# A 32-byte pad behind one small gate tile, so that every tile placed after it starts at a multiple of 64 bytes

## Chip, cores and metric

The kernel runs on one core of a Trainium2 chip. The metric is the device time of one execution in microseconds; less is better.

## The reference, cut to what matters

Three stages run one after the other on float32 data: block-causal attention, a mixture of experts whose gate is normalised by eight rounds of row and column scaling, and a "soft" mixture with 4 slots for each of 8 experts.

```python
scores = scale * np.matmul(q, k.transpose(0, 1, 3, 2))          # 4 x 8 heads, 576 x 64
attn = softmax over the allowed 64-blocks; x = attn @ v          # x becomes 2304 x 512
...
P = np.exp(logits)                                               # logits = x @ w_gate, 2304 x 8
for _ in range(8):
    P /= P.sum(1, keepdims=True) + 1e-09
    P /= P.sum(0, keepdims=True) + 1e-09
    P *= N / E
for e in range(E):
    out += P[:, e:e + 1] * (np.maximum(x @ w1[e], 0.0) @ w2[e])  # w1: 512 x 1024, w2: 1024 x 512
...
slot_input = softmax over tokens(x @ phi).T @ x                  # 32 slots
slot_out[e] = np.maximum(slot_input[e] @ w1[e], 0.0) @ w2[e]
result = softmax over slots(x @ phi) @ slot_out
```

## The kernel before

**Precision.** Matmul operands are split in two: a value rounded to the fp32r type (name ending in h) and the rest (ending in l). A product is three matmuls, h by h, h by l and l by h, into one PSUM tile.

**Stages.** Attention for 16 head pairs comes first, and the first expert matmuls fill its gaps (`fill`). The experts are cut into 32 units u of 256 hidden columns. Units 0 to 3 go plainly (`L1` at L173 to L175, `L2` at L196). For units 4 to 30 a loop at L928 runs per unit:

- `L1S` twice, for the token chunks (0, 1) and (2, 3) of 512 tokens: the first layer by a scheme with seven products instead of eight. Each product is six matmuls of 512 columns at L832. In the trace they write `A..` or `S..` and read as moving operand either tiles of x (`xh`, `xl`) or the sums of x tiles that were formed once, `T..`. Three of the seven products, S2 by T2, S3 by T3 and A22 by T4, read `T`. The stationary operand is the prepared weight tile `es`.
- `L1P` for chunk 4 of 256 tokens: 24 matmuls of 256 columns at L880 to L882.
- `L2` for all 18 token tiles: six matmuls of 512 columns each at L196. The moving operand is the weight tile `w2h` or `w2l`, the stationary one 128 tokens of the hidden tiles `hh` and `hl`. There are two sets of hidden tiles, hA in pool `ua` and hB in pool `pb`. Chunks 0, 2 and 4 use hA, chunks 1 and 3 use hB. The result is added into `acc` by VectorE at L212.

`inter` (L889) weaves these by a written pattern: pieces of `L1S` or `L1P` of the present step between pieces of `L2` of the step before. Unit 31 goes the same way, and its second layer is woven with the third stage.

**Where tiles lie.** SBUF is given out pool by pool, and every tile takes a multiple of 32 bytes on a partition. Pool `gp` holds `P` (576 bytes), `m1` (32), `rs` (96) and `cs` (32). The pools opened later lie behind it: those of the attention stage, and, in the same place once attention is over, pool `pb`. The addresses in the compiled program:

| tiles | first byte | remainder by 64 |
|---|---|---|
| xh, xl (moving at L832, L880 to L882) | 4352 to 73984 | 0 |
| w1h, w1l, w2h, w2l, also used for es | 78080 to 110848 | 0 |
| hh, hl of set hA | 114944, 119040 | 0 |
| acc of chunks 0 to 2 | 123136 to 143616 | 0 |
| P, cs | 147712, 148416 | 0 |
| pool pb: acc of chunks 3 and 4 | 148448 to 156640 | 32 |
| pool pb: T (12 tiles), tmp | 160736 to 222176 | 32 |
| pool pb: hh, hl of set hB | 193504, 197600 | 32 |
| attention: kh, kl, qs, PT, v, pe | 158560 to 209632 | 32 |

The slices that the matmuls take of these tiles start a multiple of 512 bytes behind the tile's start in all of `xh`, `xl`, `T`, `es`, `w2` and `hh`, so that they keep the remainder.

Of the kernel before, what the change touches and what calls it, by code (L numbers as in the profile page):

```python
# [7 lines left out]
F32 = mybir.dt.float32  # L8
# [9 lines left out]
N, DM, E, F = 2304, 512, 8, 1024  # L18
# [16 lines left out]
def attn_moe_softmoe_kernel(ctx: ExitStack, tc: tile.TileContext, qk1, q, k, v, wg, w1, w2, phi, m2w1, m2w2, cst, out):  # L35
# [5 lines left out]
    gp = ctx.enter_context(tc.tile_pool(name="gp", bufs=1))  # L41
# [227 lines left out]

    m1 = gp.tile([128, 1], F32, name="m1")  # L270
    rs = gp.tile([128, NT], F32, name="rs")
    cs = gp.tile([128, E], F32, name="cs")
    gl = {}
    mbt = [None]

# [1082 lines left out]
```

## Time and profile before

| | us |
|---|---|
| median of 3 runs | 1843.0 |
| lowest and highest | 1839.62, 1845.62 |
| the profiled execution, its own time | 1843.25 |
| its span in the profile | 1841.5 |

The span runs from the first to the last instruction of the profiled execution; the time lies 1.75 us above it. The mean granted clock of TensorE was 0.994 of full speed. In the chain of work a piece's duration is the time that it adds to the chain, from one start to the next; the "mean ns of one" of the groups is the span of a single matmul in the pipeline and overlaps with its neighbours.

### The profile page before, as it was taken

The numbers are of one execution on the slowest core, as the hardware profiler recorded it, in microseconds if no ns is written. First come the engines' busy times: TensorE is split into PE (matmuls) and PEld (weight loads), VectorE is DVE, ScalarE is ACT, GpSimd is POOL, SyncE is SP. The second block draws the span as 40 slices with busy tenths as digits, with TensorE's granted clock in tenths as the row PEclk, the third lists the DMA queues.
The fourth block names the chain that finished last, engine by engine and source line by source line (L and its number), as shares of the span: only waits on it lengthen the run. The fifth ranks groups of instructions, "written<-read, shape, count | busy, mean of one in ns | idle before, by whom it ended". The sixth has DMA issues, their size and how long they took to land.

```text
span 1841.5 us, 24675 instructions
## 1 busy us (share of the span) xinstructions
PE 1801.7 (98%) x9239; PEld 1443.7 (78%) x9239; DVE 1257.5 (68%) x2469; ACT 578.9 (31%) x1475; POOL 300.6 (16%) x416
## 2 busy tenths in 40 slices
PE   6999999998999999999999999999999999999997
PEld 4777777777888888888888888888888888888764
DVE  7878777479766666666666666666667666666542
ACT  4667656323222222222222222222222222222222
POOL 6546343433000000000000000000000000000010
PEclk9999999999999999999999999999999999999999
DMA  5533322010000000000000000000000000000877
GB/s 182 155 113 109 98 78 72 24 41 29 23 23 24 23 24 23 21 16 23 23 24 23 24 24 23 24 23 23 23 24 23 16 20 23 23 24 23 296 269 273
DMA packets 81095, 108.23 MB, mean 59 GB/s; under 512 B 4688, under 2 KB 55632, under 8 KB 80976
## 3 DMA queue, kind: packets, MB, share of 16 engines
q1 hardware_dynamic: 80976, 106.66, 17.8%
q8 instruction: 73, 1.20, 0.3%
q14 instruction: 46, 0.38, 0.1%
HBM read 101.92 MB, written 4.72 MB: 58 GB/s over the span
## 4 chain that ended last, share of the span: by engine, by line
PE 91%; DVE 4%; DMA 2%; POOL 1%; ACT 1%; issue 1%; SPq 0%; ACTq 0%; POOLq 0%; DVEq 0%
PE l L196 42%; PE S L832 17%; PE A L832 12%; PE pvp L551 3%; PE l L882 2%; PE l L880 2%; PE l L881 2%; PE tp L519 1%; PE l L173 1%; PE l L175 1%; PE l L174 1%; DMA r<-in_moe_w_dram 1%; PE s L442 1%; PE h L1177 1%; PE s L443 1%
## 5 line engine op out<-in xcount | busy, mean ns | idle before, releaser
L212 DVE SCALAR_TENSOR_TENSOR acc<-l,P,acc 128x512 f32<-128x512 f32 x504 | 378.1, 750 | 222.6 <-PE l L196 221.2
L196 PE MATMUL l<-w2h,hl 128*128 128x512 f32 x1132 | 446.5, 394 | 6.1 <-DVE hl L836 5.6
L196 PE MATMUL l<-w2h,hh 128*128 128x512 f32 x1132 | 451.7, 399 | 0.6 <-ACT hh L177 0.6
L196 PE MATMUL l<-w2l,hh 128*128 128x512 f32 x1132 | 446.9, 395 | 0.0
L847 DVE TENSOR_TENSOR tmp<-S,tmp 128x512 f32<-128x512 f32 x275 | 185.0, 690 | 144.4 <-PE S L832 141.4
L196 PEld LDWEIGHTS l<-w2h,hl 128*128 128x128 f32 x1132 | 213.4, 189 | 56.9 <-DVE hl L836 5.8
L196 PEld LDWEIGHTS l<-w2h,hh 128*128 128x128 f32 x1132 | 214.1, 189 | 45.5 <-ACT hh L177 1.0
L196 PEld LDWEIGHTS l<-w2l,hh 128*128 128x128 f32 x1132 | 213.7, 189 | 41.8
L835 ACT ACTIVATE hh<-tmp 128x512 fp32r<-128x512 f32 x216 | 136.6, 632 | 302.4 <-DVE tmp L847 269.8
L806 POOL TENSOR_TENSOR st<-r 128x256 f32<-128x256 f32 x56 | 40.6, 746 | 1032.6 <-DMA r<-in_moe_w_dram 1032.6
L832 PE MATMUL S<-T,es 128*128 128x512 f32 x660 | 171.8, 396 | 0.0
L832 PE MATMUL A<-xh,es 128*128 128x512 f32 x440 | 154.2, 391 | 0.0
L832 PE MATMUL S<-xh,es 128*128 128x512 f32 x440 | 154.1, 391 | 0.0
L836 DVE SCALAR_TENSOR_TENSOR hl<-tmp,hh 128x512 fp32r<-128x512 f32 x216 | 147.9, 685 | 0.1
L832 PEld LDWEIGHTS S<-T,es 128*128 128x128 f32 x660 | 124.0, 188 | 29.0
L694 ACT ACTIVATE es<-r 128x256 fp32r<-128x256 f32 x112 | 46.4, 417 | 228.0 <-PE l L881 227.2
L694 ACT ACTIVATE es<-st 128x256 fp32r<-128x256 f32 x112 | 46.4, 414 | 214.0 <-PE S L832 132.1
L832 PEld LDWEIGHTS S<-xh,es 128*128 128x128 f32 x440 | 82.6, 188 | 18.6
L119 ACT ACTIVATE w2h<-r 128x256 fp32r<-128x256 f32 x160 | 54.2, 407 | 136.1 <-PE l L196 127.4
L832 PEld LDWEIGHTS A<-xh,es 128*128 128x128 f32 x440 | 82.6, 188 | 18.0
L847 DVE TENSOR_TENSOR tmp<-A,tmp 128x512 f32<-128x512 f32 x110 | 75.9, 690 | 18.3 <-PE A L832 16.6
L832 PE MATMUL S<-xl,es 128*128 128x512 f32 x220 | 86.3, 392 | 0.0
(239 smaller groups left out, 2786.7 us busy)
## 6 DMA issues: line engine op xcount, KB each, us to landing
r<-in_moe_w_dram SPq DMA_DIRECT2D x80, 512.0 KB, 3.5
mw<-in_moe_w_dram SPq DMA_DIRECT2D x64, 512.0 KB, 6.6
kraw<-in_k_dram SPq DMA_DIRECT2D x16, 576.0 KB, 3.9
qraw<-in_q_dram SPq DMA_DIRECT2D x16, 576.0 KB, 4.3
v<-in_v_dram SPq DMA_DIRECT2D x16, 256.0 KB, 3.0
out_dram<-ob SPq DMA_DIRECT2D x6, 512.0 KB, 3.1
qk<-in_qk_dram SPq DMA_DIRECT2D x4, 512.0 KB, 6.9
out_dram<-ob SPq DMA_DIRECT2D x6, 256.0 KB, 2.3
```

The lines of the kernel that those rows point to most:

```text
L119: p = [nc.scalar.activation(out=h, in_=r[:, a:a + 256], func=AF.Copy)]
L196: nc.tensor.matmul(o, lh, w[:, kf, :], start=(m == 0), stop=(m == 5))
L212: nc.vector.scalar_tensor_tensor(out=av, in0=o, scalar=P[:, tt, e:e + 1], in1=av, op0=ALU.mult, op1=ALU.add)
L551: nc.tensor.matmul(o[64 * a:64 * a + 64, lo:hi], w, r(a), start=(m == 0), stop=(m == len(its) - 1))
L694: nc.scalar.activation(out=h, in_=src, func=AF.Copy),
L806: nc.gpsimd.tensor_tensor(out=o, in0=a, in1=b, op=alu)
L832: nc.tensor.matmul(o[:, 0:H_], a[:, k], b[:, k], start=(k == 0 and m == 0), stop=(k == 1 and m == 2))
L835: nc.scalar.activation(out=h, in_=src, func=AF.Relu)
L836: nc.vector.scalar_tensor_tensor(out=lo, in0=src, scalar=0.0, in1=f32(h), op0=ALU.max, op1=ALU.subtract)
L847: nc.vector.tensor_tensor(out=out, in0=o, in1=i, op=ALU.add)
L880: nc.tensor.matmul(o[:, 0:n], wh, xhv, start=(kt == 0), stop=False)
L881: nc.tensor.matmul(o[:, 0:n], wh, xlv, start=False, stop=False)
```

## The change

The tile `cs` is allocated with 16 instead of 8 float32 columns, and the kernel uses the first 8. It takes 64 instead of 32 bytes, so that every tile allocated behind it starts 32 bytes later. The remainder by 64 becomes 0 for all tiles of the last four rows of the table. No instruction, no order and no size of an operand is changed.

```diff
     m1 = gp.tile([128, 1], F32, name="m1")
     rs = gp.tile([128, NT], F32, name="rs")
-    cs = gp.tile([128, E], F32, name="cs")
+    cs = gp.tile([128, 2 * E], F32, name="cs")[:, 0:E]
     gl = {}
```

## Rows read from the trace of the kernel before

**Rows 1.** The page: busy time and share of the span of TensorE.
```profile
PE 1801.7 (98%) x9239; PEld 1443.7 (78%) x9239; DVE 1257.5 (68%) x2469; ACT 578.9 (31%) x1475; POOL 300.6 (16%) x416
```

**Rows 2.** The page: the chain that ended last, by engine.
```profile
PE 91%; DVE 4%; DMA 2%; POOL 1%; ACT 1%; issue 1%; SPq 0%; ACTq 0%; POOLq 0%; DVEq 0%
```

**Rows 3.** Windows: width, then busy time of each engine, PEclk, DMA share, GB/s.
```profile
440.00:450.00 10.00, 8.04 (x39) 6.57 (x37) 10.00 (x11) 3.06 (x6) 6.66 (x6) 1.00 0.16 52
450.00:455.00 5.00, 1.32 (x3) 1.13 (x4) 5.00 (x8) 0.96 (x2) 3.63 (x4) 0.57 0.00 0
...
600.00:1000.00 400.00, 400.00 (x1840) 330.17 (x1839) 275.67 (x460) 95.66 (x204) 24.07 (x33) 1.00 0.07 22
```

**Rows 4.** Waits of PE: us in total, times, longest.
```profile
PE l L196 <- DVE hl L836: 5.6, 1, 5.6
```

**Rows 5.** Chain of work through one unit, 907.40 to 954.55: start, us, what.
```profile
907.40 1.39 PE A L832 x6
908.78 1.40 PE S L832 x6
910.18 1.37 PE l L196 x6
911.55 1.40 PE S L832 x6
912.96 1.39 PE l L196 x6
914.34 1.36 PE S L832 x6
915.70 2.76 PE A L832 x12
918.46 1.39 PE S L832 x6
919.85 1.36 PE A L832 x6
921.21 1.40 PE S L832 x6
922.61 2.75 PE l L196 x12
...
929.50 1.37 PE S L832 x6
930.87 2.79 PE l L196 x12
...
937.82 1.40 PE A L832 x6
939.22 1.39 PE S L832 x6
940.61 0.12 PE l L880
...
941.32 2.75 PE l L196 x12
...
948.24 2.80 PE l L196 x12
...
954.55 1.39 PE A L832 x6
```

**Rows 6.** Groups by line and shape: busy us, mean ns of one, idle before.
```profile
L212 DVE SCALAR_TENSOR_TENSOR acc<-l,P,acc 128x512 f32<-128x512 f32 x504 | 378.1, 750 | 222.6 <-PE l L196 221.2
...
L832 PE MATMUL S<-T,es 128*128 128x512 f32 x660 | 171.8, 396 | 0.0
...
L832 PE MATMUL S<-xh,es 128*128 128x512 f32 x440 | 154.1, 391 | 0.0
...
L832 PE MATMUL A<-T,es 128*128 128x512 f32 x330 | 86.0, 396 | 0.0
...
L443 PE MATMUL s<-kl,qs 128*128 128x512 f32 x32 | 12.9, 402 | 0.0
```

## Prediction

> **What bounds the kernel now.** Read the busy shares first: TensorE is busy for 98% of the span, VectorE for 68% [rows 1]. A busy share alone doesn't say that TensorE sets the end, so the chain that ended last comes next: 91% of it lies on TensorE [rows 2]. The windows say where. Between 600 and 1000 us TensorE is busy for 400.00 of 400 us, VectorE for 275.67, and DMA takes 0.07 of its engines [rows 3]. In this long stretch nothing but the rate of back-to-back matmuls counts. At the changeover near 450 us it is another matter: VectorE is busy throughout, TensorE for 1.32 of 5 us [rows 3], and the one long wait of the second layer, 5.6 us, falls on VectorE [rows 4].
>
> A change that moves addresses alone can act only through the time of single instructions, so the last view is the chain through one unit, piece by piece [rows 5]. All its pieces of 512 columns are six matmuls or twelve, and still they don't take the same time. The reader is to sort them by the remainder of the operands' addresses. The settled best is 1.36 us for six (914.34 and 919.85, both on x tiles), 226.7 ns a matmul. The pieces that read T, whose tiles begin 32 bytes past a multiple of 64, take 1.40 us (908.78, 911.55, 921.21, 937.82, one more alike, and the second half of the piece at 915.70). Twelve matmuls with a stationary operand out of hB, which lies off by 32 too, take 2.79 or 2.80 (930.87, 948.24, and one more of each), while twelve out of hA take 2.75 even in the worst places. Pieces whose own operands are aligned, but which follow a piece that reads T or hB, take 1.37 to 1.39 (907.40, 910.18, 912.96, 918.46, 939.22, 954.55): the disturbance wears off over some six matmuls.
>
> The groups say the same of one matmul: 396 ns where T is read, 391 where xh is [rows 6].
>
> **How much an offset costs, and what it looks like.** 1.40 less 1.36 over six is 6.7 ns a matmul. Between a matmul of 256 columns, 0.12 us (940.61), and one of 512, 226.7 ns, lie 107 ns, 0.417 ns a column. So 6.7 ns is the time of 16 columns, 64 bytes of float32. A row of 512 columns is 2048 bytes; read in pieces of 64 bytes it touches 32 from an aligned start and 33 from 32 bytes past it. That is an inference from these rows; they show only the price.
>
> [...]
>
> **The change, part by part.** It adds and removes no instruction. What it moves is the start of everything in pool pb and of the attention tiles, to remainder 0.
>
> *One unit.* I put the settled time on every piece that is now disturbed, and let pieces alone whose disturbance has another cause. Such a cause is there: hA pieces right behind matmuls of 256 columns take 2.75 instead of 2.72 (941.32 and one more), with aligned operands on both sides. The hB pieces in the same place (948.24 and one more) should then fall from 2.80 to 2.75 and not to 2.72. The terms:
> - six pieces that read T, 1.40 to 1.36: 6 x 0.04 = 0.24 us;
> - hB in the first place (930.87 and one more), 2.79 to 2.72: 0.14;
> - hB behind 256 columns, two pieces: 0.10;
> - aligned pieces behind T: 910.18 0.01, 912.96 0.03, 918.46 0.03, 939.22 0.03, and two pieces of twelve (922.61 and one more, 2.75 to 2.72) 0.06, in all 0.16;
> - aligned pieces behind or ahead of hB: 907.40 0.03, 929.50 and one more 0.01 each, in all 0.05.
>
> The sum is 0.69 us of the unit's 47.15 (907.40 to 954.55).
>
> *All units.* The loop has 27 such units: 27 x 0.69 = 18.6 us. As a check, 660 and 330 matmuls read T [rows 6], that is 165 pieces of six, 27.5 units' worth. Unit 31 has its six T pieces as well, with followers: 0.24 + 0.16 = 0.4 us.
>
> *Does it reach the end?* In this stretch TensorE has no gaps that could swallow it [rows 3]. What is late next is VectorE: it has 275.67 of 400 us to do, and with TensorE 1.5% faster 394 us for it, 70%. The adds into acc take 750 ns [rows 6] for every six second-layer matmuls, half of the 1.36 us that those take. VectorE, ScalarE and GpSimd get no time credited.
>
> *Attention.* Its score matmuls read kh, kl and qs, all off by 32. Only the 64 of 512 columns (L442 and L443, 32 each) can be set beside a like shape: 402 ns against 391 [rows 6], 64 x 11 ns = 0.7 us. The other 320 are narrower; from below they gain nothing, from above 11 ns each, 3.5 us. TensorE isn't alone on the chain there, and the changeover behind it hangs on VectorE [rows 3, 4]; I take 0.5 us for the stage, nearer to the lower end, and keep 0 and 4.2 for the range.
>
> *Sum.* 18.6 + 0.4 + 0.5 = 19.5 us off the profiled execution's 1843.25: 1823.75. The median of the runs is 0.25 us lower than that execution, so 1823.5 us, 1.06% less.
>
> **The rivals.**
>
> *The pieces are slow for where the tiles lie, not for the remainder.* All slow tiles lie at 148448 bytes or above, and every fast fp32r operand of 512 columns lies below, so the trace can't part the two by itself. Against it: the excess is the time of 64 bytes, and T tiles spread over 62 kB show the same 1.40. If it holds, the time stays at 1843.2 us, give or take 3. [...]
>
> *Only one of the two operands matters for its remainder.* T is moving, hB is stationary. If only T gains, a unit gives 0.24 + 0.16 = 0.40 us, and 27 units 10.8: with unit 31's 0.4 the time is 1831.8. If only hB does, 0.14 + 0.10 + 0.05 = 0.29 a unit, 7.8 us: 1835.2. For it speaks that the two enter by different reads; against it that both show the same excess, 2.80 less 2.75 where the place is the same and 1.40 less 1.36.
>
> *Slower: the clock gives way in the long stretch.* At the changeover the granted clock fell to 0.57 in a 5 us window in which TensorE was busy for 1.32 us [rows 3]; so a fall by half is to be had in this kernel. From 600 to 1000 us it is 1.00. [...] From (19.5 + 5.5) x 2 = 50 us of lower clock on, the kernel would be measurably slower, 1849 us or more. Against it: TensorE is already busy throughout that stretch, at full clock.
>
> **How the numbers follow.** This kernel can show a difference of 0.3%, 5.5 us. I give the full gain 0.80, the gain of one operand alone 0.10, no change 0.06, the clock 0.04. The first two are faster by more than 5.5 us, so faster is 0.90, same 0.06, slower 0.04. The range: at the low end attention gives its 4.2 instead of 0.5 us, 1843.0 - 18.6 - 0.4 - 4.2 = 1819.8, and 1819 with the rounding of the pieces; at the high end it takes in the case that only T gains, 1832, and 1833 with the same allowance. Both together hold some 8 in 10, since the full case can also miss by more than the pieces' rounding (0.005 us in each of some 20 pieces of 27 units, up to 2.7 us if all err the same way).
>
> **What would show it right or wrong.** In the chain through one unit: the pieces that read T at 1.36, those of hB at 2.72 and, behind 256 columns, 2.75, those behind T at 1.36, the unit at about 46.46 us. The group of S on T at 391 ns instead of 396. VectorE's adds into acc still at 750 ns. T pieces still at 1.40 would make the remainder the wrong cause; hB at 2.79 beside T at 1.36 would mean that only the moving operand counts; a unit of 46.46 and a time that hasn't fallen by some 19 us would mean that the gain is lost at the changeover or behind unit 31.

## The result, and the profile after

The changed kernel takes 1824.14 us in the median of 4 runs (1821.59 to 1826.4), the kernel before 1843.57 beside it. The ratio is 0.9897, with a 95% interval of 0.9873 to 0.992: 1.0% faster. The forecast was 1823.5 us.

The chain of work through one unit of the changed kernel, 897.90 to 944.38 us (start, us, what); it answers to [rows 5]:

```profile
897.90 1.36 PE A L832 x6
899.26 1.36 PE S L832 x6
...
904.70 1.36 PE S L832 x6
906.06 2.72 PE A L832 x12
...
912.86 2.72 PE l L196 x12
...
921.02 2.72 PE l L196 x12
...
927.82 1.36 PE A L832 x6
...
931.25 2.75 PE l L196 x12
...
938.17 2.75 PE l L196 x12
...
944.38 0.68 PE A L832 x3
```

Every piece of six in this unit takes 1.36 us now, with T or without (899.26 and 927.82 read T), every piece of twelve 2.72, with hA (912.86) or hB (921.02). Behind matmuls of 256 columns both take 2.75 (931.25 hA, 938.17 hB). The unit lasts 46.48 us instead of 47.15.

The groups by line and shape of the changed kernel, against [rows 6] (busy us, mean ns of one, idle before):

```profile
L212 DVE SCALAR_TENSOR_TENSOR acc<-l,P,acc 128x512 f32<-128x512 f32 x504 | 377.9, 750 | 212.8 <-PE l L196 212.4
...
L832 PE MATMUL S<-T,es 128*128 128x512 f32 x660 | 167.3, 389 | 0.0
...
L832 PE MATMUL S<-xh,es 128*128 128x512 f32 x440 | 153.3, 389 | 0.0
...
L443 PE MATMUL s<-kl,qs 128*128 128x512 f32 x32 | 12.8, 401 | 0.0
```

T and xh are alike at 389 ns (391 was forecast; the matmuls on xh that follow T were disturbed before and are in that mean), VectorE's add is unmoved at 750, and so, all but 1 ns, is the score matmul of the attention stage (402 before).

The span fell by 21.7 us, to 1819.8, more than the medians did. Three lines of each chain say where: the 30 second-layer matmuls near 384 us, the first A piece of the loop, and the first of unit 31. Before:

```profile
384.06 9.47 PE l L196 x30
...
462.24 1.39 PE A L832 x6
...
1709.00 1.39 PE A L832 x6
```

After:

```profile
384.17 6.93 PE l L196 x30
...
459.15 1.39 PE A L832 x6
...
1688.06 1.36 PE A L832 x6
```

The loop, from its first A piece to unit 31, takes 1228.91 us instead of 1246.76, 17.85 less, and what comes behind takes 0.8 less. The other 3.1 us were gained ahead of the loop, 2.5 of them by the 30 matmuls (6.93 instead of 9.47). That is the clock, in the windows from 380 us on, before and after (width, busy times, PEclk, DMA share, GB/s):

```profile
380.00:390.00 10.00, 6.84 (x21) 5.38 (x21) 7.29 (x19) 2.36 (x7) 3.95 (x4) 0.66 0.08 29
```

```profile
380.00:390.00 10.00, 6.74 (x33) 5.56 (x32) 8.79 (x22) 2.36 (x7) 4.27 (x4) 1.00 0.11 41
```

The first of these two is of before. There the clock granted was 0.66 in that stretch: 0.50 from 384 to 388 us, after TensorE had waited for 3.16 us, with a matmul of 512 columns started every 0.426 us. This execution of the changed kernel kept 1.00 behind a wait of 3.26 us, with one every 0.227, and why isn't shown. It is the fastest of its four runs; the medians, 19.4 us apart, don't rest on it.

### The profile page after: what moved, and what is told of

Same layout as the page of the kernel before. It is cut to its first block, busy times and chain, and to the rows that moved or that the text cites. A ratio compares the mean times of both kernels' runs of the same rounds, so it can differ in the third digit from the quotient of the medians.

```text
span 1819.8 us, 24675 instructions
## 1 busy us (share of the span) xinstructions
PE 1779.8 (98%) x9239; PEld 1441.5 (79%) x9239; DVE 1255.9 (69%) x2469; ACT 579.4 (32%) x1475; POOL 301.7 (17%) x416
## 4 chain that ended last, share of the span: by engine, by line
PE 89%; DVE 3%; POOL 1%; DMA 1%; ACT 1%; issue 1%; SPq 0%; ACTq 0%; DVEq 0%; POOLq 0%
PE l L196 42%; PE S L832 16%; PE A L832 12%; PE pvp L551 2%; PE l L882 2%; PE l L881 2%; PE l L880 2%; PE l L173 1%; PE tp L519 1%; PE l L175 1%; DMA r<-in_moe_w_dram 1%; PE l L174 1%; PE h L1177 1%; PE s L442 1%; PE s L443 1%
## 5 line engine op out<-in xcount | busy, mean ns | idle before, releaser
L832 PE MATMUL S<-T,es 128*128 128x512 f32 x660 | 167.3, 389 | 0.0
L832 PE MATMUL A<-xl,es 128*128 128x512 f32 x220 | 85.6, 389 | 0.0
```

The lines of the kernel that those rows point to most:

```text
L832: nc.tensor.matmul(o[:, 0:H_], a[:, k], b[:, k], start=(k == 0 and m == 0), stop=(k == 1 and m == 2))
```

## The experiments

In all of them "lower tiles" are x, the weights with es, and hA; "upper tiles" are T, tmp and hB. Unless it is said otherwise, the edit is shown against the changed kernel. Remainders by 256 are those of the tiles' addresses in the compiled programs.

### Upper tiles 64 bytes past a multiple of 128

```diff
-    cs = gp.tile([128, 2 * E], F32, name="cs")[:, 0:E]
+    cs = gp.tile([128, 4 * E], F32, name="cs")[:, 0:E]
```

> The pad is 96 bytes instead of 32, so that T, hB and the attention tiles start 64 bytes past a multiple of 128 (in the changed kernel all of them start at multiples of 128). Theory (a piece of 64 bytes is what counts): T pieces 1.36 us, hB 2.72 and 2.75, unit 46.48, time 1822 to 1826. Rival (the boundary is 128 bytes): T pieces 1.40, hB 2.79 to 2.80, unit about 47.15, time about 1843.

Measured: 1844.53 us, ratio to before 1.0008 (0.9999 to 1.0017). All upper tiles start at multiples of 64, and nothing is gained. Chain:

```profile
908.08 1.39 PE A L832 x6
909.47 1.39 PE S L832 x6
...
931.61 2.80 PE l L196 x12
```

The piece on T (909.47) takes 1.39, that on hB (931.61) 2.80; the unit 47.20. So in this kernel a multiple of 64 is not enough, against the prediction's reading. 128 was the rival written down; the next pair of runs shows that it isn't a multiple of anything that is wanted.

### Lower tiles off, and all tiles off

```diff
-    wg_raw = const.tile([128, KD, E], F32, name="wg_raw")
+    wg_raw = const.tile([128, KD * E + 8], F32, name="wg_raw")[:, 0:KD * E].rearrange("p (k e) -> p k e", k=KD)
```

This puts 32 bytes ahead of all lower tiles. With `cs` at its old 32 bytes the upper ones come to lie at multiples of 256, to the same addresses as in the changed kernel; with `cs` at 64 bytes every operand of the long stretch starts 32 past one.

> The mirror image: a 32-byte pad in the first pool and none at cs. Now x, w1, w2, es and the hidden tiles hA start 32 bytes past a multiple of 64, T and hB (and the attention tiles) at multiples. Theory A (one disturbance per matmul, whether one operand is off or both): every matmul of 512 columns takes 1.40/6, a unit 192 x 6.7 ns = 1.28 us more than 46.48, with 0.16 for the 24 matmuls of 256 columns 47.9, time about 1824 + 39 = 1863. Theory B (the prices of the two operands add): pieces with both off, S, A on x tiles and second layer on hA, 1.44; unit about 48.6, time about 1881. Rival (it is the upper addresses that are slow): unit 46.48 or less, 1824.

> Pad of 32 bytes in the first pool and 64 bytes for cs: all operands of the fp32r matmuls start 32 bytes past a multiple of 64, moving and stationary. Theory A (one disturbance per matmul): the same as with the low tiles off, all pieces 1.40, unit 47.9, about 1863. Theory B (prices add): all pieces 1.44, unit 49.2 with the matmuls of 256 columns, about 1897.

Measured: with the lower tiles off 1843.31 us, ratio 1.0001 (0.9992 to 1.001); with all off 1825.56 us, 0.9905 (0.9891 to 0.9918). Both theories written down forecast 1863 us or more for both, and both fell; so did the rival of the upper addresses, 1824 us with the lower tiles off. The chain with all operands 32 bytes past a multiple of 64:

```profile
907.38 1.36 PE S L832 x6
...
922.34 1.36 PE S L832 x6
923.70 2.72 PE l L196 x12
...
940.85 2.75 PE l L196 x12
```

No disturbed piece is left, and the unit takes 46.48, as with every operand at a multiple of 64. With the lower tiles alone off:

```profile
909.60 1.40 PE S L832 x6
911.00 1.37 PE l L196 x6
...
931.69 2.79 PE l L196 x12
```

Here T and hB lie at multiples of 64, and their pieces are the slow ones again, in the same places and by the same amounts; the unit is 47.15 to the digit. The offset of an operand alone explains neither kernel. What the slow pieces share is that moving and stationary operand start at different remainders: T against es, w2 against hB.

### A constant difference, everywhere

All stationary operands are put off, all moving ones left at multiples of 256 (the tiles made 128 bytes larger and read from 32 bytes on). As the tiles grew by 128 bytes, the stationary operands lie 32 past a multiple of 256 in some of the tiles and 160 past one in the others; within a piece at L834 it is one of the two throughout.

```diff
+    def h_new(hp, tag, name):
+        return hp.tile([128, 1056], F32R, tag=tag, name=name)[:, 8:1032].rearrange("p (k f) -> p k f", k=2)
...
-            es[i] = wp.tile([128, 2, 2, 2, 128], F32R, tag=ETAG[i], name=f"es{i}")
+            es[i] = wp.tile([128, 1056], F32R, tag=ETAG[i], name=f"es{i}")[:, 8:1032].rearrange("p (j s k f) -> p j s k f", j=2, s=2, k=2)
```

> Changed kernel, with every stationary operand of the long stretch (es, and the hidden tiles of both sets) 32 bytes past a multiple of 128, every moving one (x, T, w2) at a multiple. Theory A (the difference between the moving operand and the stationary one counts, in every matmul): all six-piece times 1.40, twelve 2.80, unit 46.48 + 192 x 0.0067 = 47.8 and more with the matmuls of 256 columns, time 1860 to 1865. Theory B (only a change of remainder from one matmul to the next disturbs, and a constant difference is free): all 1.36 and 2.72, unit 46.48, about 1825.

Measured: 1857.27 us, 1.0068 (1.0053 to 1.0083), slower than before. The chain (two lines of code more, so L834 and L198):

```profile
910.66 1.40 PE A L834 x6
...
917.66 1.40 PE S L834 x6
...
926.05 2.80 PE l L198 x12
...
948.49 2.79 PE l L198 x12
```

All pieces are slow, those on x tiles (917.66) as those on T, although every moving operand is aligned. The unit takes 47.63, 1.15 more than in the changed kernel; the loop from its first A piece to unit 31 takes 30.6 us more, of the 33 between the two medians. The difference inside a matmul's pair of operands counts, not a change from one matmul to the next. The forecast of 47.8 was high because pieces behind 256 columns, at 2.75 already, rose by less than twelve times 6.7 ns.

### How large the period is

The pad puts the upper tiles 128 past a multiple of 256, where the lower ones are at multiples of 256.

```diff
-    cs = gp.tile([128, 2 * E], F32, name="cs")[:, 0:E]
+    cs = gp.tile([128, 6 * E], F32, name="cs")[:, 0:E]
```

> The theory of 64-byte pieces has fallen: all tiles off by 32 ran as fast as all aligned, and upper tiles 64 past a multiple of 128 ran as slow as before. New theory: what counts is whether the moving and the stationary operand start at the same remainder by some power of two; 64 apart is slow, and 256 apart is fast (in the changed kernel the lower tiles lie at 256 by 512 and the upper ones at 0). Here the pad puts the upper tiles 128 past a multiple of 256, the lower ones at multiples of 256. Period 128: T 1.36, hB 2.72 and 2.75, unit 46.48, 1822 to 1826. Period 256: T about 1.39 to 1.40, hB 2.79 to 2.80, unit about 47.1, about 1843.

Measured: 1839.37 us, 0.9978 (0.9967 to 0.9988). Chain:

```profile
907.87 1.39 PE S L832 x6
...
929.87 2.80 PE l L196 x12
...
950.75 2.77 PE l L196 x12
953.52 1.36 PE A L832 x6
```

T takes 1.39, hB 2.80 or 2.77, the unit 47.01: 128 apart is disturbed, a little less than 32 or 64 apart. In the changed kernel the lower tiles start at remainder 256 by 512 and the upper ones at 0, and nothing is disturbed. So 256 apart is free, and of the powers of two tried the period is 256 bytes.

### T alone, hB alone, and a mistake in both

```diff
-        Tf[p, j] = tuple(pb.tile([128, 2, H_], F32R, tag=..., name=...) for d in range(2))
+        Tf[p, j] = tuple(pb.tile([128, 2 * H_ + 16], F32R, tag=..., name=...)[:, 8:2 * H_ + 8].rearrange("p (k f) -> p k f", k=2) for d in range(2))
```

> Changed kernel, with the T tiles alone read 32 bytes past a multiple of 64 (16 columns more in each tile, the first 8 left free); hB aligned. Theory (either operand's remainder costs, each by itself): T pieces 1.40, pieces behind them 1.36 to 1.39, hB 2.72 and 2.75, unit 46.48 + 0.40 = 46.9, time about 1824 + 11 = 1835. Rival (only the stationary operand counts): T pieces 1.36, time 1824.

> Changed kernel, with the hidden tiles of set hB alone 32 bytes past a multiple of 64; T aligned. Theory: hB pieces 2.79 and 2.80, T pieces 1.36, unit 46.48 + 0.29 = 46.8, time about 1824 + 8 = 1832. Rival (only the moving operand counts): hB 2.72 and 2.75, time 1824.

Measured: T 1839.29 us, 0.998 (0.9971 to 0.999); hB 1835.99 us, 0.9959 (0.9945 to 0.9973). Both are slower than forecast, by 4 us each. These two ran before the period was known, and their larger tiles (64 bytes more) moved what lies behind: in the first run hB came to 128 past a multiple of 256, in the second T of the chunks 2 and 3 did. The edited tiles moved one another too: T lies 32, 96, 160 and 224 past one in the first, hB 32 and 96 in the second. The chain shows it, of the kernel with T off first:

```profile
908.68 1.39 PE S L832 x6
...
930.70 2.80 PE l L196 x12
```

```profile
907.79 1.36 PE S L836 x6
...
920.03 1.39 PE S L836 x6
...
929.65 2.79 PE l L200 x12
```

In the first, hB is slow too (930.70), though it starts at a multiple of 64. In the second, where lines stand four further down, T is free in the half of the unit for chunks 0 and 1 (907.79) and slow in the half for chunks 2 and 3 (920.03).

The second was done again with tiles 256 bytes larger, so that only hB differs:

```diff
+        return hp.tile([128, 1088], F32R, tag=tag, name=name)[:, 8:1032].rearrange("p (k f) -> p k f", k=2)
```

> The changed kernel with hB alone 32 bytes off once more, but with each of its two tiles 256 bytes larger, not 64, so that every other tile of the long stretch keeps the remainder 0 by 256. In the earlier run the tiles behind hB were put 128 past a multiple of 256, and T of the chunks 2 and 3 with them. Theory (what counts is the difference of moving and stationary operand by 256): T pieces 1.36 throughout, hB 2.79 and 2.80, pieces next to hB 1.37 to 1.39, unit 46.48 + 0.29 = 46.77, time about 1824 + 8 = 1832. Rival (something else in the larger hB tiles slowed T in the earlier run): T of one half of the unit still at 1.39 to 1.40, unit about 46.9 and time about 1836.

Measured: 1832.41 us, 0.9936 (0.9923 to 0.995). Chain of one unit, 857.50 to 904.26:

```profile
857.50 1.38 PE A L836 x6
858.88 1.36 PE S L836 x6
...
871.12 1.36 PE S L836 x6
...
880.65 2.79 PE l L200 x12
...
904.26 1.38 PE A L836 x6
```

T is free in both halves (858.88, 871.12), hB slow, the unit 46.76 where 46.77 was forecast, and the time within 0.4 us of it. A clean run with T alone was not made.

### Smaller differences

T 16 and hB 48 bytes off, by the edit above with other offsets and 64 bytes more in each tile; then 16 bytes in both, with 128 bytes more.

> Changed kernel, with T read 16 bytes and hB 48 bytes past a multiple of 64. Theory (a row that doesn't start on a 64-byte boundary touches one piece more, whatever the offset): as in the kernel before, T pieces 1.40, hB 2.79 to 2.80, unit about 47.15, time about 1842. Rival (the price goes with the offset, or only a 32-byte half matters): T at 16 bytes about half, 1.38, hB at 48 bytes 1.5 times, 2.83 and 2.83; unit 47.15 - 0.20 + 0.15. Rival (any multiple of 16 is free): unit 46.48, time 1824.

> Changed kernel, with T (moving) and hB (stationary) 16 bytes past a multiple of 128, all else at multiples. If any difference costs the full price: T 1.40, hB 2.79 to 2.80, unit 47.15, 1843. If the price grows with the difference, as the mixed run with T at 16 and 80 bytes and hB at 48 and 112 suggests: T 1.37 to 1.39, hB 2.74 to 2.77, unit between 46.6 and 47.0, time 1828 to 1838.

Measured: 1837.95 us, 0.9963 (0.995 to 0.9976), unit 46.94; and 1834.25 us, 0.9947 (0.993 to 0.9963), unit 46.83. Neither is clean, for the reason just told: in the first, T lies 16, 80, 144 and 208 past a multiple of 256 and hB 176 and 240, in the second both lie 16 and 144 past one. The chain of the second:

```profile
908.02 1.39 PE S L836 x6
...
927.25 2.72 PE l L200 x12
...
944.45 2.79 PE l L200 x12
```

T takes 1.39, and the hB pieces 2.72 in one place (927.25) and 2.79 in another (944.45), with the same tiles and so the same differences. So the price isn't a function of the difference alone; the run-up counts too, and how it goes with a small difference stays open. That a multiple of 16 bytes is free is refuted by both.

### The attention tiles

```diff
-        qraw = ap1.tile([128, 1280], F32, name="qraw")
+        qraw = ap1.tile([128, 1288], F32, name="qraw")[:, 0:1280]
```

> Changed kernel, with the attention tiles alone back at 32 bytes past a multiple of 64 (a pad in their first tile); T and hB aligned. The prediction gave attention 0.5 us of the gain and bounded it by 0 and 4.2. Theory after the result: nothing, the last score matmul starts at 332 us with either, unit 46.48, time 1824. Rival: attention ends 0.5 to 4 us later.

Measured: 1822.34 us (1820.74 to 1824.09), 0.9886 (0.9872 to 0.9899), unit 46.48: no loss against 1824.14, the runs overlap. The last score matmul starts at 332.28 us, as forecast, but in the changed kernel's profile at 335.00 and before at 334.73, so that "with either" is a miss, in the direction of no loss; what the 2.7 us come from isn't known. The stage gains nothing from the change that these runs can tell. The operands of its score matmuls of 512 columns moved together: kh, kl and qs all start 96 past a multiple of 256 before, 128 in the changed kernel and 160 here, which by the theory of differences is no disturbance between them in any of the three.

### Fewer switches from 256 to 512 columns

The entry 16 of the patterns for the 256-column step, cut out of its line:

```diff
-... 16: "ppllllppllllppllllppllll"
+... 16: "ppppllllllllppppllllllll"
```

In this order the hidden values of chunk 4 are written over those of the first 256 tokens of chunk 2 before the second layer has read them, so part of the computation runs on other values.

> Changed kernel, with the pattern of the 256-column step written with two switches from 256 to 512 columns where there are four. What is left above 2.72 for twelve matmuls stands behind such switches (2.75). Theory: two pieces of twenty-four at 5.47 instead of four of twelve at 2.75, unit 46.48 - 0.06 = 46.42, 1.6 us less over 27 units, too little for the time to show. Rival: VectorE or ScalarE falls behind in the longer runs and TensorE waits, unit longer than 46.48.

Measured: 1828.47 us (1825.14 to 1830.82), 0.9919 (0.9905 to 0.9932), not less than the changed kernel. The unit is 46.60, longer. Chain:

```profile
934.35 5.61 PE l L196 x24
...
941.39 5.47 PE l L196 x24
```

The second piece of 24 takes the forecast 5.47, the first 0.14 us more. In the first, weight loads wait (the last figures are the idle time before them and what ended it):

```profile
935.11 0.19 PEld L196 LDWEIGHTS l<-w2h,hh 128*128 128x128 f32 x1 [0.27 <-ACT hh L835]
...
935.60 0.19 PEld L196 LDWEIGHTS l<-w2h,hl 128*128 128x128 f32 x1 [0.19 <-DVE hl L836]
```

They wait for the hidden values of chunk 4 that ScalarE and VectorE have just written, 256 columns each, from 934.70 us on. So the longer unit comes from the order itself, which makes the second layer read what was written a moment before, and not, as the rival had it, from VectorE or ScalarE falling behind. What fewer switches would bring without that wait was not measured. No version was found that is faster than the changed kernel by more than the spread of the runs.

## Why the prediction was right, and where its reason was not

**What bounds the kernel: right.** TensorE is busy for 400 of 400 us from 600 to 1000 us in the changed kernel as well, and the long stretch gave its gain to the end undiminished: 17.85 us in the loop, 0.8 more behind it.

**Which pieces are disturbed, and by how much: right.** A unit gained 0.67 us where the sum had 0.69. The pieces came out as listed, those on T at 1.36, those on hB at 2.72 and 2.75, followers at 1.36. The reading rested on sorting one unit's pieces and on taking the best piece as the price of all.

**How many units: slightly wrong.** The loop was taken as 27 such units, with unit 31 besides. But unit 4, its first, runs `L1S` for the chunks 0 and 1 alone and sends 2, 3 and 4 through `L1P` (`["3", "2", "4", 0] if u == 4`), other than the section on the kernel before says of units 4 to 30. So 26 units of the loop are like the one shown, and the 27.5 units' worth of T pieces that the prediction counted as a check have unit 31 in them already. From the loop on the sum had 19.0 us; measured are 18.6.

**Luck.** With that and without the 0.5 us for attention the sum would have been some 18.6 us, 0.8 less than the 19.4 between the medians. That rest is well inside the spread of the four runs (1821.59 to 1826.4), and that the forecast came within 0.7 us of the median is partly luck.

**What an offset costs and what it looks like: wrong.** This step read 6.7 ns as one more piece of 64 bytes touched, and the remainder by 64 as its cause. Three runs refute it: upper tiles at another multiple of 64 are as slow as before (1844.53), all tiles off by 32 as fast as the changed kernel (1825.56), and lower tiles off, upper aligned, is the kernel before in the mirror (unit 47.15). The runs showed in its place that the moving and the stationary operand are undisturbed where their start addresses differ by a multiple of 256 bytes: 1.36 us for six and a unit of 46.48, in the changed kernel and with all tiles off by 32. Before, the lower tiles lay at 0 and the upper at 224 by 256; the pad of 32 brought both to 0. That 0 is also a multiple of 64 is by the way.

**Why a wrong reason gave the right number.** In the long stretch of this kernel every operand with remainder 0 by 64 had also remainder 0 by 256, and every other one 224. The trace of before could not tell an offset from a difference. The settled price was read from rows and didn't depend on the reason; a forecast for another pad by the same reason would have failed, as the first expectation above did.

**The rivals.** The place in the upper addresses: refuted by the result, since T and hB still lie above 148448 and their pieces are settled, and by the mirror run, where they lie at the very addresses of the changed kernel and are slow. One operand alone: in the form given it falls too, since each matters only against the other; hB off by itself costs 8 us (1832.41 against 1824.14). The clock did not give way in the long stretch: the granted clock is 1.00 from 600 to 1000 us. The factor of 2 in that rival's 50 us was the author's estimate; the matmuls at a granted clock of 0.50 near 384 us followed each other every 0.426 us instead of every 0.227, 1.9 times as long.

**Attention: sized wrong.** 0.5 us was given for it, none is seen: 401 ns a score matmul after 402, and no loss with its tiles put back. Its rows were set beside aligned ones of another place in the chain. The operands of these matmuls started at the same remainder by 256 before as well, so the 11 ns between the rows had another cause, which was not traced.

**Open.** Why the period is 256 bytes, why the disturbance lasts some six matmuls, and why a switch from 256 to 512 columns disturbs like a difference in address were not settled; nor why, with differences of 16 and 144 bytes, the same hB pieces are free in one place and slow in another. Weight loads run beside the matmuls (in the changed kernel 334.92 us of them from 600 to 1000 us, where TensorE multiplies for all 400); that the disturbance arises there is the author's guess, and no run shows it.

## What to carry to other kernels

Where back-to-back fp32r matmuls are the bound, print the start addresses of moving and stationary tiles and compare them by 256 bytes before touching anything else: here a difference of 32 cost 6.7 ns in each matmul of 512 columns, and one odd tile of 32 bytes ahead of a pool, which put everything behind it off, 19.4 us of 1843.57. Sort equal matmuls of one iteration by their time and by every property of their operands, differences between operands among them, and don't take the first property that sorts them for the cause. An experiment that enlarges a tile moves all that lies behind it: keep its size a multiple of the largest period in question.

## What the runs showed of the hardware that was not expected

- fp32r matmuls of 512 columns follow each other every 226.7 ns (1.36 us for six) where moving and stationary operand start at the same remainder by 256 bytes (0 and 0 in the changed kernel, 32 and 32 with all tiles off), and every 233 ns (1.40) where they differ by 32 (0 and 224 before). Differences of 64 and 128 cost nearly as much (2.80 for twelve, in places 2.77; units of 47.20 and 47.01 us beside 47.15); a difference of 256 costs nothing (unit 46.48).
- VectorE's adds show no such effect: 750 ns before and after, with the tiles of chunks 3 and 4, a third of the adds, moved by the pad.
- A switch from matmuls of 256 to those of 512 columns costs 0.03 us in the next twelve (2.75 against 2.72) with all operands alike.
